# An attention and token/channel mixer on one core: the relative-position bias rectified on one side and read in both directions, rows shifted by the DRAM pitch, and a new order

## The chip, the core and the metric

One core of one Trainium2 chip runs the kernel. The time is the device time of one execution in microseconds; the runs shown are three, and their median is used. A separate execution was profiled.

## The reference, cut to what matters

```python
def _attn_ref(q, k, v, w1, b1, w2):            # (4, 8, 576, 64); hidden 32
    scores = scale * np.matmul(q, k.transpose(0, 1, 3, 2))
    rel = (pos[:, None] - pos[None, :]).astype(np.float32)
    psi_rel = np.log1p(np.abs(rel))
    psi_i = np.log1p(np.maximum(pos[:, None].astype(np.float32), 1.0))
    x = (psi_rel / psi_i)[..., None]
    h = np.maximum(x @ w1 + b1, 0.0)
    bias = h @ w2
    scores = scores + bias.transpose(2, 0, 1)[None, :, :, :]
    scores = scores - np.max(scores, axis=-1, keepdims=True)
    attn = np.exp(scores)
    attn = attn / (np.sum(attn, axis=-1, keepdims=True) + 1e-09)
    return np.matmul(attn, v).astype(np.float32)

def _moe_ref(x, w_tok1, w_tok2, w_ch1, w_ch2): # x: the attention, (4, 576, 512)
    h = np.maximum(x.transpose(0, 2, 1) @ w_tok1, 0.0) @ w_tok2
    u = x + h.transpose(0, 2, 1)
    h2 = np.maximum(u @ w_ch1, 0.0) @ w_ch2
    return (u + h2).astype(np.float32)
```

The bias depends on the row i, on the distance |i - j| and on the head, and on nothing else: for one row it is a function of the distance alone, so the values left of the diagonal are those to the right of it, mirrored.

## The kernel before

**The opening** draws the bias. A table `lw` of log1p(distance), repeated over 128 partitions (4 rows x 32 hidden units), is 1148 columns wide and holds both sides of the diagonal. The 576 x 576 x 8 bias is made in 36 blocks of 16 query rows. For each block four `rectify` steps (L487; L492 on ScalarE, L494 on VectorE) each write 576 columns for four query rows: relu(w1 x log + b1 x psi_i). One of the four goes to ScalarE and three to VectorE. Eight fp32 products of 32 x 288 (L511) apply w2 and put 16 rows x 8 heads on 128 partitions of a PSUM pair; the step `over` (L517) divides by psi_i and copies 576 columns to SBUF, and `put` (L522) sends them to a DRAM tile `bd` (one for each 128 query rows). Beside this, the eight loads of v (L538) and ten products with each (L545) measure v for its scale, the token weights, which come in 64-bit words, are decoded by steps on VectorE (L630, L635, L359), GpSimd (L632, L638) and ScalarE (L634), and k and q are split in a high part (L369, ScalarE) and a rest (`kl`, `ql`, L384, GpSimd).

**Attention** is 16 units (4 pairs of heads, `hp`, by 4 batches) of 5 chunks of query rows. A chunk's scores are products (L783); VectorE adds the bias and takes the row's extreme (L792, the "biased z"); ScalarE takes the exponential (L805); the result is turned by TensorE (L834) with copies of high part and rest (L837, L840), or, for some chunks, split by `rest_hi` (L815, ScalarE) and `rest_lo` (L819 and L384, GpSimd) and turned by a transposing DMA (L823); products with v follow (L861 to L863), then the norm and the token mix, whose stores are L940 (`um`) and L942 (`ul`). The bias of a pair of heads is loaded by `bias_load` (L716 for the four full chunks, L719 twice for the last), once for its four units. The loads of qT, kT (L741) and v (L745) of the next unit are issued by ScalarE's queue, the others by SyncE's.

**The channel part** follows from some 350 us on; the change touches none of its code.

**The order** of all steps is written by a planner, `Plan.order`. It lists for each engine the steps whose inputs are there, takes the engine that could start first, and of the steps that could start within `SLACK` of that the one with the smallest due time (`DUE`); a step in TensorE's present mode gets `STAY` off its due time. `ON` holds costs and preferences for steps that more than one engine can do. The engines then run their instructions in that order, each its own, and wait for one another by semaphores. When TensorE would stand idle in the plan, the planner puts in warming products (L318). DMAs take their semaphores from a ring of eight, so that a DMA is issued only when the one eight before it has landed.

The steps of a block in the opening, as the planner gets them:

```python
rs = [add({"A": 0.68} if g == 3 else {"V": 0.47}, t + DUE["rect"], rectify(hs, g, q0 + 4 * g, 4 * n + g), after=[room], port=True) for g in range(4)]
...
m = add({"T": 1.05}, t + DUE["bmm"], mm, after=rs, take=[ph], free=[hs], mode=3)
...
v_ = add(ON["over"], t + DUE["over"], over, after=[m], take=[eh], free=[ph])
```

## Time and profile before

| | us |
|---|---|
| median of 3 runs | 644.96 |
| lowest, highest | 642.58, 646.78 |
| profiled execution, its own time | 641.31 |
| its span in the profile | 639.4 |
| TensorE busy | 617.8 |
| VectorE busy | 501.8 |
| ScalarE busy | 410.0 |
| GpSimd busy | 266.4 |

The span runs from the first to the last instruction that the profiler shows; 1.9 us of the execution's own time lie around it. An engine's busy time is the union of its instructions, without the issuing of DMAs. A share over the whole span says little here, since the opening, the attention and the channel part have different limits; the stretches have to be read one by one. Rows name the tiles by the program's names; `slots` and `rect` are large tiles that hold many things in turn, so that "rect" in an attention row is a buffer for z. A releaser in brackets is the instruction that ended the idle time before the row.

### The profile page before, as it was taken

The numbers are of one execution on the slowest core, as the hardware profiler recorded it, in microseconds if no ns is written. First come the engines' busy times: TensorE is split into PE (matmuls) and PEld (weight loads), VectorE is DVE, ScalarE is ACT, GpSimd is POOL, SyncE is SP. The second block draws the span as 40 slices with busy tenths as digits, with TensorE's granted clock in tenths as the row PEclk, the third lists the DMA queues.
The fourth block names the chain that finished last, engine by engine and source line by source line (L and its number), as shares of the span: only waits on it lengthen the run. The fifth ranks groups of instructions, "written<-read, shape, count | busy, mean of one in ns | idle before, by whom it ended". The sixth has DMA issues, their size and how long they took to land.

```text
span 639.4 us, 18066 instructions
## 1 busy us (share of the span) xinstructions
PE 617.8 (97%) x7226; PEld 457.3 (72%) x7226; DVE 501.8 (78%) x1242; ACT 410.0 (64%) x751; POOL 266.4 (42%) x299
## 2 busy tenths in 40 slices
PE   9999888998999999999999999999999999999997
PEld 4445777896999998989899874444444468646886
DVE  7998899987899999999999867994775894266222
ACT  7998888876798999989888525542542641244110
POOL 1004777953575888778653700001233422022211
PEclk9999999998999999999999999999999999999999
DMA  8999665798676965466544795664221115400221
GB/s 314 403 365 336 132 143 146 264 332 191 192 160 194 287 125 138 112 144 185 132 95 86 240 290 213 180 176 116 52 64 40 63 34 132 99 1 0 81 86 33
DMA packets 88515, 101.92 MB, mean 159 GB/s; under 512 B 49392, under 2 KB 58864, under 8 KB 88432
## 3 DMA queue, kind: packets, MB, share of 16 engines
q1 hardware_dynamic: 78784, 80.04, 44.6%
q10 hardware_dynamic: 9648, 20.75, 11.1%
q8 instruction: 56, 0.92, 0.6%
q14 instruction: 27, 0.22, 0.1%
HBM read 69.69 MB, written 20.05 MB: 140 GB/s over the span
## 4 chain that ended last, share of the span: by engine, by line
PE 72%; DVE 9%; ACT 7%; DMA 5%; POOL 4%; issue 3%; ACTq 0%; SPq 0%; POOLq 0%; DVEq 0%
PE pair L783 7%; PE bank L834 6%; PE bank L1103 5%; PE bank L1104 5%; PE bank L1102 5%; PE bank L1289 4%; PE bank L1287 4%; PE bank L1288 4%; PE pair L511 4%; DVE z L792 3%; DVE t2a L840 2%; PE pair L1104 2%; PE bank L1195 2%; PE bank L1194 2%; PE pair L1103 2%
## 5 line engine op out<-in xcount | busy, mean ns | idle before, releaser
L805 ACT ACTIVATE z<-z,mx 128x576 f32<-128x576 f32 (+1 forms) x120 | 92.7, 780 | 12.1 <-DVE mx L792 7.6
L792 DVE CUSTOM_DVE_ANT_0 z<-pair,slots 128x576 f32<-128x576 f32 (+1 forms) x120 | 89.3, 756 | 4.2 <-PE pair L783 3.6
L840 DVE SCALAR_TENSOR_TENSOR t2a<-bank,t2a 128x384 f16<-128x384 f32 (+1 forms) x150 | 79.6, 538 | 6.6 <-ACT t2a L837 5.1
L834 PE MATMUL bank<-id,z 128*128 128x128 f32 x469 | 76.0, 283 | 6.2 <-DVE t2a L840 2.7
L837 ACT ACTIVATE t2a<-bank 128x384 f16<-128x384 f32 (+1 forms) x150 | 70.2, 473 | 16.8 <-PE bank L834 11.2
L783 PE MATMUL pair<-kh,qh 64*128 64x288 f32 (+1 forms) x288 | 62.5, 347 | 4.7 <-DVE mx L792 4.0
L834 PEld LDWEIGHTS bank<-id,z 128*128 128x128 f32 x469 | 50.0, 141 | 15.8 <-issue 4.8
L1103 PE MATMUL bank<-slots 128*128 128x512 f16 (+1 forms) x168 | 58.6, 349 | 1.3 <-DMA slots<-wd 1.3
L861 PE MATMUL bank<-vh,t2a 128*128 128x65 f16 x558 | 58.6, 194 | 0.0
L1102 PE MATMUL bank<-slots 128*128 128x512 f16 (+1 forms) x168 | 58.6, 349 | 0.0
L1104 PE MATMUL bank<-slots 128*128 128x512 f16 (+1 forms) x168 | 58.6, 349 | 0.0
L863 PE MATMUL bank<-vh,t2a 128*128 128x65 f16 x558 | 58.2, 192 | 0.1
L862 PE MATMUL bank<-vl,t2a 128*128 128x64 f16 x558 | 58.3, 191 | 0.0
L1298 DVE SCALAR_TENSOR_TENSOR slots<-bank,crow,slots 128x256 f32<-128x256 f32 x42 | 19.6, 481 | 43.2 <-PE bank L1289 34.2
L783 PE MATMUL pair<-kl,qh 64*128 64x288 f32 (+1 forms) x288 | 52.6, 299 | 0.0
L1232 POOL TENSOR_TENSOR me<-me 128x512 f32<-128x512 f16 x12 | 13.6, 1152 | 92.9 <-DVE wd L1078 76.2
L862 PEld LDWEIGHTS <-t2a 128*128 128x128 f16 x558 | 51.2, 98 | 0.6 <-issue 0.2
L861 PEld LDWEIGHTS <-t2a 128*128 128x128 f16 x558 | 51.1, 97 | 0.4 <-issue 0.2
L863 PEld LDWEIGHTS <-t2a 128*128 128x128 f16 x558 | 51.1, 97 | 0.2 <-DVE t2a L840 0.2
L783 PE MATMUL pair<-kh,ql 64*128 64x288 f32 (+1 forms) x288 | 50.9, 292 | 0.0
L783 PEld LDWEIGHTS pair<-kh,qh 64*128 64x128 f32 (+1 forms) x288 | 34.6, 185 | 16.8 <-DVE mx L792 7.6
L1104 PEld LDWEIGHTS <-slots 128*128 128x128 f16 x240 | 23.5, 98 | 24.7 <-issue 1.6
(271 smaller groups left out, 2037.2 us busy)
## 6 DMA issues: line engine op xcount, KB each, us to landing
keep<-wc SPq DMA_DIRECT2D x24, 512.0 KB, 4.2
wd<-wc SPq DMA_DIRECT2D x24, 512.0 KB, 4.7
bd<-slots SPq DMA_DIRECT2D x36, 288.0 KB, 6.4
slots<-bd SPq DMA_DIRECT2D x16, 576.0 KB, 6.9
slots<-v SPq DMA_DIRECT2D x8, 640.0 KB, 8.8
tv<-v ACTq DMA_DIRECT2D x16, 320.0 KB, 3.8
qq<-qT ACTq DMA_DIRECT2D x16, 320.0 KB, 4.2
kk<-kT ACTq DMA_DIRECT2D x16, 320.0 KB, 4.6
```

The source lines that it names most:

```text
L783: PE.matmul(out=pairs[both[h].i][:, 512 - i + n * i:512 + n * i], lhsT=qx[x][w, c * 128:c * 128 + 128], rhs=kx[y][w, k0:k0 + i], start=(j ...
L792: V.tensor_tensor_reduce(out=st["z"][z.i][:, o], in0=pairs[ph.i][:, 512 - i:512 + i], in1=bias_m[hp][:, c, h, :] if c < NCH else bias_l[hp ...
L805: A.activation(out=zz, in_=zz, func=ACTF.Exp, bias=mx_t[z.i][:, h:h + 1], scale=-1.0)
L834: PE.transpose(banks[tb.i][:, n * 128:(n + 1) * 128], st["z"][z.i][:, 384 * i + n * 128:384 * i + (n + 1) * 128], id32)
L837: A.activation(out=block(h.i, 0, m), in_=banks[tb.i][:, 0:128 * m], func=ACTF.Copy, scale=P_SCALE)
L840: V.scalar_tensor_tensor(out=block(h.i, 3, m), in0=banks[tb.i][:, 0:128 * m], scalar=P_SCALE, in1=block(h.i, 0, m), op0=ALU.mult, op1=ALU. ...
L861: PE.matmul(out=o, lhsT=lh, rhs=vh[:, n, 0:D + 1], start=(i == 0), stop=False)
L862: PE.matmul(out=ps[:, h, 0:D], lhsT=lh, rhs=vl[:, n, :], start=False, stop=False)
L863: PE.matmul(out=o, lhsT=ll, rhs=vh[:, n, 0:D + 1], start=False, stop=(i == 4))
L1102: PE.matmul(out=ps, lhsT=w[0][:, c], rhs=uh[:, c], start=(c == 0), stop=False)
L1103: PE.matmul(out=ps, lhsT=w[0][:, c], rhs=ul[:, c], start=False, stop=False)
L1104: PE.matmul(out=ps, lhsT=w[1][:, c], rhs=uh[:, c], start=False, stop=(c == 3))
```

## The change

- `rectify` writes only `far = max(q0 + 16, 576 - q0)` columns, from distance 0 up: the longer of the two sides of the diagonal. The table `lg` is 576 wide and no longer 1148.
- The products read the columns to the right of the diagonal forwards and those to the left of it backwards (step -1), from the same rectified tile. Each row group writes 591 columns (`FOLD`), in which row i of the 16 stands shifted by i columns. A block has cuts at the place where the direction turns and at the border of the PSUM bank: 8 products in 28 blocks, 12 in the other 8.
- `over` copies 591 columns and `put` writes 128 rows of 591 at a pitch of 608 elements. The shift of a row is undone by the load: `bias_rows` reads with a row pitch one element shorter, two pieces of 576 elements for a partition in place of one of 1152.
- v comes a second time, unpadded (`vr`), for its scale: 1152 columns for 1280, nine products for ten.
- The planner counts the ring of eight (`lands`), lets the scores of the first two chunks go ahead of the last product of the bias (`drawn`), and gets new costs, due times, `SLACK` and `STAY`; so the order of all steps is new.

```diff
-TAB = 1148
+FOLD = S + 15
+BP = 608
+BR = NH * BP
-SLACK = 0.099
-STAY = 136.61
+SLACK = 0.095
+STAY = 406.23
...
-       'put': -1632.04,
-       'bl': 332.43,
+       'put': -3146.07,
+       'bl': 136.34,
...
-        wire, port, port_by = 4.0, 0.0, None
+        wire, port, port_by, lands = 4.0, 0.0, None, [0.0] * 4 + [4.0] * 4
...
+                    if s.wire:
+                        t = max(t, lands[0])
...
+                lands = lands[1:] + [s.end]
...
+        def bias_rows(c, i, n, h, m):
+            t = bd[c]
+            return bass.AP(t.tensor, t.offset + 15 + i * (BR - 1) + h * BP, [[BR - 1, n], *([[BP, m]] if m > 1 else []), [1, S]])
...
-        def rectify(h, g, q, k):
+        def rectify(h, g, n, k):
             def do(e):
-                r, win = rect_t[4 * h.i + g], lw[:, 572 - q:572 - q + S]
+                r, win = rect_t[4 * h.i + g][:, 0:n], lw[:, 0:n]
...
-            rs = [add({"A": 0.68} if g == 3 else {"V": 0.47}, t + DUE["rect"], rectify(hs, g, q0 + 4 * g, 4 * n + g), after=[room], port=True) for g in range(4)]
+            far = max(q0 + 16, S - q0)
+            rs = [add({"A": 0.16 + 0.52 * far / S} if g == 3 else {"V": 0.17 + 0.3 * far / S}, t + DUE["rect"], rectify(hs, g, far, 4 * n + g), after=[room], port=True) for g in range(4)]
...
-                for x in range(2):
+                cuts = sorted({0, back_, 512 - w0, FOLD})
+                for a, b in zip(cuts, cuts[1:]):
                     for g in range(4):
-                        PE.matmul(out=pairs[ph.i][NF * g:NF * g + NF, 224 + 288 * x:512 + 288 * x], lhsT=wf.rearrange("p g h -> p (g h)"),
-                                  rhs=rect_t[4 * hs.i + g][:, 288 * x:288 * x + 288], start=True, stop=True)
+                        x = rect_t[4 * hs.i + g]
+                        x = bass.AP(x.tensor, x.offset + abs(a - back_), [x.ap[0], [-1 if a < back_ else 1, b - a]])
+                        PE.matmul(out=pairs[ph.i][NF * g:NF * g + NF, w0 + a:w0 + b], lhsT=wf.rearrange("p g h -> p (g h)"), rhs=x, start=True, stop=True)
...
-                x, y = pairs[ph.i][:, 224:800], eb_t[eh.i]
+                x, y = pairs[ph.i][:, w0:w0 + FOLD], eb_t[eh.i]
...
-                ENG[e].dma_start(out=bd[c][16 * o:16 * o + 16].rearrange("q (h j) -> (q h) j", j=S), in_=eb_t[eh.i])
+                ENG[e].dma_start(out=bass.AP(bd[c].tensor, bd[c].offset + 16 * o * (BR - 1), [[BP, 128], [1, FOLD]]), in_=eb_t[eh.i])
...
-                        for k in range(10):
+                        for k in range(9):
...
-                                      lambda e, c=c: ENG[e].dma_start(out=slots[:, hp % 2, c * PW:(c + 1) * PW], in_=bd[c][:, hp * PW:(hp + 1) * PW]), after=[*bias_s[c], *after])]
+                                      lambda e, c=c: ENG[e].dma_start(out=slots[:, hp % 2, c * PW:(c + 1) * PW].rearrange("p (h j) -> p h j", h=2), in_=bias_rows(c, 0, 128, 2 * hp, 2)), after=[*bias_s[c], *after])]
...
-                lead = chain("scores", add({"T": 0.9 if c < NCH else 0.95}, t + DUE["scores"], scores, after=[*ready, *bias_in[hp, c], drawn],
+                lead = chain("scores", add({"T": 0.9 if c < NCH else 0.95}, t + DUE["scores"], scores, after=[*ready, *bias_in[hp, c], *([drawn] if u or c > 1 else [])],
...
-                    s = add({"A": 0.45}, t + DUE["hi"], rest_hi, after=exps[:1], take=[p2], use=[z])
+                    s = add({"A": 0.45}, t + DUE["hi"], rest_hi, after=[exps[0], drawn], take=[p2], use=[z])
```

In this diff, `back_ = q0 + 15` is the number of columns read backwards, and `w0` the place in the PSUM pair where the 591 columns begin. How the instructions of three places stood and stand follows; the lines of the new file are a few higher (L522 is L535, L716 is L729, L719 is L732, L940 is L953, L632 is L645, L638 is L651, L384 is L389, L819 is L832).

SyncE's queue toward the end of the opening, before: `bd_132` to `bd_136` are the five DRAM tiles of the bias, a row from `slots` is a put (or so many), a row to `slots` a load of the first pair of heads.

```order
L522 DMA bd_133<-slots 128x576 x6
L522 DMA bd_134<-slots 128x576 x4
L716 DMA slots<-bd_132 128x1152
L522 DMA bd_134<-slots 128x576
L716 DMA slots<-bd_133 128x1152
L522 DMA bd_134<-slots 128x576 x3
L522 DMA bd_135<-slots 128x576 x5
L716 DMA slots<-bd_134 128x1152
L522 DMA bd_135<-slots 128x576 x3
L522 DMA bd_136<-slots 128x576 x4
L716 DMA slots<-bd_135 128x1152
```

The same place now:

```order
L535 DMA bd_134<-slots 128x591
L370 DMA keep<-wt 128x1024
L535 DMA bd_135<-slots 128x591 x8
L535 DMA bd_136<-slots 128x591 x2
L729 DMA slots<-bd_132 128x2x576
L535 DMA bd_136<-slots 128x591
L729 DMA slots<-bd_133 128x2x576
L729 DMA slots<-bd_134 128x2x576
L535 DMA bd_136<-slots 128x591
L729 DMA slots<-bd_135 128x2x576
```

The first load of the bias (`bd_132`) stood behind 20 puts, and now stands behind 34 of the 36; the others follow it closely.

GpSimd's queue about the first splits of k and q, before: `keep` is a decode's buffer, `kl_108` and `ql_110` are rests of k and q, `z_118` the first chunk's z.

```order
L611 MEMSET wt2l 128x2x64
L632 TENSOR_SCALAR keep<-keep 128x512
L384 TENSOR_TENSOR kl_108<-kk,kh_107 128x640
L384 TENSOR_TENSOR ql_110<-qq,qh_109 128x640
L819 TENSOR_SCALAR z_118<-z_118 128x384
L384 TENSOR_TENSOR rect<-z_118,rect 128x384
L638 TENSOR_TENSOR slots<-keep 128x512
```

The same place now:

```order
L624 MEMSET wt2l 128x2x64
L651 TENSOR_TENSOR slots<-keep 128x512
L389 TENSOR_TENSOR kl_108<-kk,kh_107 128x640
L645 TENSOR_SCALAR keep<-keep 128x512
L389 TENSOR_TENSOR ql_110<-qq,qh_109 128x640
L737 MEMSET slots 64x64
L738 MEMSET slots 64x64
L651 TENSOR_TENSOR slots<-keep 128x512
L439 MEMSET vh_111 128x10
L440 MEMSET vh_111 64x1
L441 MEMSET vh_111 64x1
L645 TENSOR_SCALAR keep<-keep 128x512
```

The decode step (L632) that stood right ahead of `kl_108` is now L645 and stands eight rows above the piece shown, ahead of the clearing of `vh_113`; two further decodes (L645, L651) stand between the splits and the rows of `z_118`, which come behind seven more rows of clearing (L832, L389).

SyncE's queue at the load of the third pair's bias and the stores of the first token mixes (`um`, `ul`), before:

```order
L823 DMA_TRANSPOSE rect<-rect 128x6x128 x2
L365 DMA keep<-wc 128x1024
L716 DMA slots<-bd_132 128x1152
L716 DMA slots<-bd_133 128x1152
L716 DMA slots<-bd_134 128x1152
L716 DMA slots<-bd_135 128x1152
L719 DMA slots<-bd_136 64x576 x2
L940 DMA um_127<-x_84 128x4x128
L942 DMA ul_130<-x_84 64x128
```

The same place now:

```order
L836 DMA_TRANSPOSE rect<-rect 128x6x128
L729 DMA slots<-bd_132 128x2x576
L729 DMA slots<-bd_133 128x2x576
L953 DMA um_127<-x_84 128x4x128
L955 DMA ul_130<-x_84 64x128
L729 DMA slots<-bd_134 128x2x576
L729 DMA slots<-bd_135 128x2x576
L836 DMA_TRANSPOSE rect<-rect 128x6x128
L370 DMA keep<-wc 128x1024
L732 DMA slots<-bd_136 64x576 x2
L836 DMA_TRANSPOSE rect<-rect 128x6x128
```

The store of `um_127` stood behind all six loads of this bias; now it stands behind two of them, and four come after it.

## Rows read from the trace of the kernel before

**Rows 1.** Page, part 1: busy us (share of the span) xinstructions

```profile
PE 617.8 (97%) x7226; PEld 457.3 (72%) x7226; DVE 501.8 (78%) x1242; ACT 410.0 (64%) x751; POOL 266.4 (42%) x299
```

**Rows 2.** Stretches (start:end, length, then busy PE, PEld, DVE, ACT, POOL, PEclk, DMA, GB/s)

```profile
0.00:57.00 57.00, 53.38 (x692) 26.21 (x692) 50.19 (x120) 52.73 (x80) 2.81 (x18) 1.00 0.97 356
57.00:100.00 43.00, 38.87 (x531) 32.83 (x532) 38.06 (x106) 35.39 (x67) 34.25 (x56) 1.00 0.67 177
100.00:147.00 47.00, 44.16 (x699) 39.68 (x699) 42.98 (x123) 38.32 (x73) 32.60 (x41) 1.00 0.81 256
147.00:157.00 10.00, 6.93 (x68) 5.36 (x68) 6.55 (x17) 6.91 (x13) 3.50 (x4) 0.83 0.95 206
157.00:200.00 43.00, 42.95 (x754) 39.26 (x751) 39.55 (x107) 35.08 (x67) 27.93 (x27) 1.00 0.69 181
...
350.00:635.00 285.00, 283.14 (x1970) 178.33 (x1966) 182.17 (x386) 105.39 (x199) 61.83 (x49) 1.00 0.37 106
```

**Rows 3.** Grouped lines by form, 0 to 60 us: busy us, mean ns

```profile
L517 ACT ACTIVATE slots<-pair,slots 128x576 f32<-128x576 f32 x36 | 26.4, 736 | 0.8 <-PE pair L511 0.2
...
L494 DVE TENSOR_SCALAR rect<-slots 128x576 f32<-128x576 f32 x54 | 24.1, 522 | 0.0
...
L511 PE MATMUL pair<-rect,slots 128*32 128x288 f32 x288 | 21.3, 410 | 1.4 <-ACT slots L517 1.2
...
L492 ACT ACTIVATE rect<-slots 128x576 f32<-128x576 f32 x18 | 13.6, 771 | 0.0
```

**Rows 4.** Timeline of ACT, 0 to 12 us (start us, us, what)

```profile
5.76 1.44 ACT L492 ACTIVATE slots<-slots 128x576 f32<-128x576 f32 x2
```

**Rows 5.** Timeline of PE, 44 to 75 us ([idle before <-releaser])

```profile
57.18 0.39 PE L783 MATMUL pair<-kh,qh 64*128 64x288 f32 x1 [0.39 <-ACT slots L517]
```

**Rows 6.** Timeline of PE, 22 to 32.5 us

```profile
25.57 0.75 PE L545 MATMUL bank<-slots 128*128 128x128 bf16 x10
26.24 2.15 PE L511 MATMUL pair<-rect,slots 128*32 128x288 f32 x32
```

**Rows 7.** DMA, 0 to 57 us (issues: xcount, KB each, median us to landing)

```profile
DMA packets 8937, 20.29 MB, mean 356 GB/s; under 512 B 870, under 2 KB 1126, under 8 KB 8928
...
bd<-slots SPq DMA_DIRECT2D x35, 288.0 KB, 6.4
...
slots<-bd SPq DMA_DIRECT2D x3, 576.0 KB, 6.5
```

**Rows 8.** Grouped lines by form, whole span: exp in two widths

```profile
L805 ACT ACTIVATE z<-z,mx 128x576 f32<-128x576 f32 x106 | 81.4, 774 | 7.6 <-DVE mx L792 7.0 <-DVE sc L596 0.3
...
L805 ACT ACTIVATE z<-z,mx 128x640 f32<-128x640 f32 x14 | 11.6, 826 | 4.5 <-DMA um<-x 3.9 <-DVE mx L792 0.6
```

**Rows 9.** Timeline of DVE, 56 to 61 us

```profile
58.24 0.76 DVE L792 CUSTOM_DVE_ANT_0 z<-pair,slots 128x576 f32<-128x576 f32 x1 [1.11 <-PE pair L783]
```

**Rows 10.** Chain that ended last, 70 to 97 us, its head by line

```profile
by line: POOL ql L384 11.5%; POOL kl L384 11.4%; POOL slots L638 11.0%; POOL vl L384 9.9%; issue 9.7%; PE pair L783 4.3%; DVE keep L630 3.9%; POOL keep L632 3.9%; DVE m L359 3.5%; DVE t2a L840 3.4%; POOL rect L384 3.4%; POOL xl L384 3.2%; P
```

**Rows 11.** Grouped lines by form, 57 to 110 us

```profile
L384 POOL TENSOR_TENSOR kl<-kk,kh 128x640 fp32r<-128x640 f32 x4 | 6.2, 1557 | 1.4 <-ACT rect L837 0.7 <-ACT t2a L837 0.5 <-ACT kh L369 0.2
...
L638 POOL TENSOR_TENSOR slots<-keep 128x512 f32<-128x512 f32 x3 | 3.5, 1162 | 0.0
...
L635 DVE SCALAR_TENSOR_TENSOR keep<-keep 128x512 int32<-128x512 int32 x3 | 2.9, 965 | 0.0
...
L632 POOL TENSOR_SCALAR keep<-keep 128x512 f32<-128x512 f32 x3 | 2.0, 661 | 1.1 <-DVE mxgv L323 1.1
```

**Rows 12.** Timeline of SP, 131 to 150 us

```profile
134.83 1.76 SPq L716 DMA_DIRECT2D slots<-bd  x4
...
138.25 0.48 SPq L940 DMA_DIRECT2D um<-x  x1
```

**Rows 13.** Chain that ended last, 136 to 152 us (start us, us, what)

```profile
138.25 10.53 DMA um<-x
```

**Rows 14.** Timeline of ACT, 146 to 150 us

```profile
149.25 0.83 ACT L805 ACTIVATE z<-z,mx 128x640 f32<-128x640 f32 x1 [3.91 <-DMA um<-x]
```

More of the change, by code (lines that the diff above doesn't have):

```diff
@@ new lines @@
+      'over': {'A': 0.65, 'V': (0.72, 1893.12)},
+      'vh': {'P': (0.7, 1744.94), 'V': (0.4, 999.31), 'A': (0.6, -572.78)},
+      'vl': {'P': (1.36, 1742.79)}}
+DUE = {'tie': 3214.81,
+       'blk': -672.54,
+       'blkn': 50.2,
+       'rect': -472.18,
+       'bmm': -2332.09,
+       'over': -3547.32,
+       'put': -3146.07,
+       'bl': 136.34,
+       'bln': 91.98,
+       'sums': 1443.85,
+       'sumsn': 290.25,
+       'measw': 61.31,
+       'measwn': 81.35,
+       'amax': 622.86,
+       'scales': 365.78,
+       'scalet': -2029.85,
+       'scalec': -785.97,
+       'fill': -1268.45,
+       'fill1': 1424.77,
+       'tok': -986.12,
+       'tokn': 12.44,
+       'dec1': -322.51,
+       'dec2': 676.98,
+       'dec3': 196.27,
+       'dec4': -28.73,
+       'dec5': -1091.05,
+       'load_k': 23.9,
+       'load_q': -1095.84,
+       'split_k': -406.91,
+       'first_k': -128.79,
+       'first_q': -446.99,
+       'split_q': -235.74,
+       'load_v': -1851.82,
+       'prep_v': 3726.37,
+       'prep_vh': -2173.87,
+       'prep_vl': -2860.64,
+       'scores': -148.81,
+       'biased': -160.4,
+       'exp': -560.33,
+       'hi': -929.4,
+       'lo': 287.58,
+       'turn': -239.45,
+       'flip': -605.86,
+       'fliphi': -1578.93,
+       'flip2': -811.41,
+       'fliplo': 61.62,
+       'back': 838.71,
+       'norm': -56.39,
+       'mix0': -1007.88,
+       'mix1': 469.44,
+       'relu': -3392.19,
+       'mix2': -2979.92,
+       'mix2b': -153.48,
+       'store': -1789.73,
+       'w1': 717.8,
+       'w1n': 176.19,
+       'U0': 1280.18,
+       'U0n': -381.53,
+       'U1n': -297.68,
+       'U1': 883.15,
+       'U2': -180.11,
+       'Un': 33.16,
+       'U3': 1371.94,
+       'U4': -465.64,
+       'u1': 1863.2,
+       'u2': -221.98,
+       'u3': -642.62,
+       'u4': -1822.27,
+       'u5': 122.46,
+       'G': 1437.72,
+       'G0': 970.16,
+       'G0n': 43.23,
+       'g1': -1521.12,
+       'g2': 155.66,
+       'ur': 717.4,
+       'H': 2474.54,
+       'e1': 154.26,
+       'e2': -579.53,
+       'e3': -870.28,
+       'e4': 432.52,
+       't2': 1433.37,
+       't3': 155.16,
+       't4': -1001.58,
+       'T1': -1499.32,
+       'Tn': -166.71,
+       'rd': 2012.78,
+       'urs': 350.87,
+       'un': 178.06,
+       'v1': -59.34,
+       'v2': 2407.34,
+       'v3': 41.73,
+       'v4': 1010.47,
+       'v5': -895.21,
+       'v6': -420.54,
+       'v7': -236.11,
+       'v8': -2263.69,
+       'w2m': -62.0,
+       'w2mn': 50.25}
@@ L527, in attention_mixer @@
             overs.append(v_)
-            bias_s.setdefault(c, []).append(add(wire("put", 0.8), t + DUE["put"], put, after=[v_], free=[eh]))
+            bias_s.setdefault(c, []).append(add(wire("put", 0.82), t + DUE["put"], put, after=[v_], free=[eh]))
             bias_all.extend(bias_s[c][-1:])
@@ L537, in load @@
                     def load(e, i=i, h=h):
[L538 removed]
+                        ENG[e].dma_start(out=staging(h.i, 2 * S), in_=vr[i])
                     def sums(e, i=i, h=h):
[L542 to L543 removed]
+                        t = staging(h.i, 2 * S).bitcast(BF16).rearrange("p (n t) -> p n t", t=2)[:, :, 1]
+                        for k in range(9):
                             x = t[:, k * 128:(k + 1) * 128]
[L545 to L547 removed]
+                            PE.matmul(out=banks[vh_.i][:, 0:128], lhsT=x, rhs=x, start=(i == 0 and k == 0), stop=(i == 7 and k == 8))
+                    x = add(wire("sums", 1.51), DUE["sums"] + DUE["sumsn"] * i, load, take=[h])
                     late.append((x, i))
[L549 removed]
+                    last = add({"T": 0.61}, DUE["sums"] + DUE["sumsn"] * i + 6, sums, after=[x, last], take=[vh_] if i == 0 else [], free=[h], use=[vh_])
                     sums_all.append(last)
```

156 lines of the change are left out of this document (26 added, 130 removed).

## The prediction

> **What bounds the kernel now.** I read the busy line of the page first: TensorE is busy 97% of the span, VectorE 78%, ScalarE 64%, GpSimd 42% [rows 1]. So little can be gained by making any other engine cheaper, unless it is the one that TensorE waits for, and the next question is where the missing 3% lie. The table by stretches answers it [rows 2]. From 157 us on TensorE idles 0.05 of 43 us, and 1.9 of the last 285 us; what lies between I take to be of the same kind. The losses are in front: 57.00 - 53.38 = 3.6 us before 57 us, 43.00 - 38.87 = 4.1 to 100 us, 2.8 to 147 us, and 3.1 in the ten microseconds from 147, in which the granted clock is 0.83 besides: a third of that stretch at the lower level (1.2 GHz) costs about 10 x (1 - 0.83) = 1.7 us more. All that a new order can win lies in these four places, some 15 us, since the work behind 157 us is the same and full.
>
> The opening (0 to 57 us) has to be read apart, because TensorE's 53.38 us there are not all work: warming products fill its pauses. In the grouped lines the scaling copy "over" costs ScalarE 736 ns, and it does one rectify of 771 ns in each block; VectorE does three of 522 ns [rows 3] (the row shown is one of two like halves each time: 36 overs, 36 rectifies on ScalarE, 108 on VectorE, 576 matmul records, two to a product). ScalarE starts rectifying at 5.76 us [rows 4] and is busy 52.73 us of the 57 [rows 2]; the first scores wait for its last "over" and start at 57.18 us [rows 5]. VectorE is nearly level (50.19 us busy). TensorE's own share is smaller: two blocks, 32 records, take 2.15 us, so 1.08 a block, and ten products of v for its scale 0.75 including what overlaps, 0.68 from start to start [rows 6]. DMA is at 0.97 in the same stretch, moving 20.29 MB at 356 GB/s [rows 2, 7]. So three resources are within some 10% of each other there, and taking work from one makes the next the bound.
>
> **The change part by part.** All of it is summed against the profiled execution: 641.31 us, of which 639.4 are the span. The median of the runs is 644.96, 3.65 more, and I add that at the end.
>
> *Opening: rectify, copy, products, v unpadded.* A block now rectifies max(q0 + 16, 576 - q0) columns, 440 of 576 in the mean over 36 blocks. ScalarE's slope comes from one line in two widths: 774 ns at 576 columns, 826 at 640 [rows 8], so 52 / 64 = 0.81 ns a column. It saves 136 x 0.81 = 0.110 us x 36 = 4.0; "over" grows by 15 columns, 0.012 x 36 = 0.4; the scaling of the halved table loses 284 columns, 0.2. Together -3.8: the last "over" ends near 53.4 us. VectorE saves in like measure. But the first biased z needs a bias load too. In the old order that load stands behind 20 puts, in the new one behind 34 of 36. Blocks leave ScalarE every (57.2 - 5.8) / 36 = 1.43 us, so the 34th "over" ends near 50.5; put and load take 6.4 to 6.5 us from issue to landing [rows 7], so the load lands near 57.0. On VectorE the first z now also stands behind parts of two decode steps, among them one more operation of 0.965 us and what waits for GpSimd. So z, which began at 58.24 us [rows 9], begins near 57.7: **-0.5**. The floor is -3 (load no longer late, z right behind the products); the ceiling +2 (two decodes of VectorE and GpSimd end first). The bytes say the same: puts grow by 36 x 128 x 15 x 4 = 0.28 MB, v falls by 0.52 and the table by 0.29, so 0.5 MB or 1.5 us at 356 GB/s is all that a DMA-bound opening could give. The 32 products more cost nothing while TensorE's end in the opening (5.8 + 36 x 1.11 + 8 x 0.61 = 50.6 us) is ahead of ScalarE's.
>
> *57 to 100 us: GpSimd's queue.* From 70 to 97 us GpSimd's lines make 54% of the chain [rows 10] (the seven lines of GpSimd that this row names, added). In the old order the splits kl and ql (1.56 us each, ql taken like kl) stand behind a decode step, L632, that VectorE holds until 57 us (the idle time of that line names the releaser, L323 [rows 11]); GpSimd is busy 2.81 us of the first 57 [rows 2]. In the new order what stands ahead of them is released earlier, so they can run inside the opening, and two further decodes (0.661 + 1.162 us each) [rows 11] stand ahead of the first residual of z, which is late anyway. That is 3.1 + 3.6 = 6.7 us less in the chain's stretch at the most; at GpSimd's share 0.54 x 6.7 = **-3.5**. Ends: 0, if the engines beside it (VectorE 38.06 and ScalarE 35.39 of 43 us) become the bound; -6.7, though only 4.1 + 2.8 us of idling can go.
>
> *147 to 157 us: the stall.* SyncE issues four bias loads and two small ones, and the store of the attention's output behind them at 138.25 us [rows 12]; that store lands 10.53 us later [rows 13], and it is what the queue of ScalarE waits for: 3.91 us before it issues the load of qT and goes on with exp [rows 14], because a DMA waits for the one eight before it. In the new order two bias loads stand ahead of that store, and the other two and the small ones behind it and a transpose. With four of six loads gone from in front, the store lands several microseconds earlier, and ScalarE's load has another DMA eight before it. The stall's price is 3.1 idle + 1.7 of clock = 4.8; I take **-4**, ends 0 (another wait of the same ring at the same place) and -4.8.
>
> *What is added.* A bias load is now 128 rows of two pieces of 2304 bytes at a pitch of 2428 and no longer one of 4608; no row shows such a load. From below it costs nothing (the same bytes, hidden behind the full TensorE); from above one stall like the 3.91 us [rows 14]. The same bound holds for the waits on the DMA ring, which the new planner counts but which land elsewhere on the chip than it assumes. I take **+1.0**, nearer to the lower end, since the same bytes are moved and the next set of bias is loaded while TensorE still works on the one before; ends 0 and +4.
>
> No row shows what a start off a boundary costs a transfer. The Trainium skill ("DMA: Bandwidth & Descriptors", section "How a descriptor splits into AXI transactions") speaks against this part: a piece that does not start on a multiple of 256 bytes begins its first transaction at the boundary below, and the bytes before it cost beats too. By it a piece of 72 beats would take about 76, so 5.5% more for 16 loads of 0.59 MB, an estimate of 1.5 us of DMA time spread over the run, most of it hidden; the sum would be +0.5 higher if a third of it showed.
>
> Sum: -0.5 - 3.5 - 4.0 + 1.0 = -7.0, so 634.3 for a profiled execution, and 634.3 + 3.65 = 638.0 against the median. The ends added (-3 - 6.7 - 4.8, and +2 + 4) give 630.5 and 651.
>
> **The rivals.** *A, the gain goes into another wait.* The opening stays bound by DMA (0.97), the moved GpSimd work only delays the first z, and a stall of the same size stands elsewhere on the ring of eight. For it: the DMA share [rows 2] and a load that stands 14 puts later. Against it: the stall was one accident in an otherwise full run. Then 0 to +2 from the opening, -3.5 or 0 behind it, and the stall kept: 641 to 648, in the middle 644.
>
> *B, the order repairs more.* If the opening gives its -3 and the idle time to 147 us falls to a third of its 6.9 us (-4.6), with the stall's -4.8 and nothing added: -12.4, so 632.6.
>
> *C, slower: reading backwards costs TensorE.* In the mean 295 of 591 columns are read with step -1. Nothing in the trace reads with a negative step. Against a price: the products of v read with step 2, at 0.068 us each for 128 columns, 0.53 ns a column [rows 6], where the opening's, at step 1, take 1.08 / 8 / 288 = 0.47; so a step by itself costs next to nothing. If a reversed column costs twice, a block is 1.08 x (591 + 295) / 576 = 1.66 us, 36 of them and 8 x 0.61 us of sums from 5.8 us on end at 70.5 us, 13.3 after the present start of the scores. Then 13.3 - 3.5 - 4 + 1 = +6.8, so 651.8. With a factor f for reversed columns TensorE's end is 50.6 + 19.9 x (f - 1): below f = 1.33 it is hidden behind ScalarE, from f = 1.66 on the kernel is slower than before.
>
> *D, the rectify doesn't shrink with its columns.* Then -3.8 becomes 0 on ScalarE, but the load decided there anyway: 639, inside the forecast's own range.
>
> **How the numbers follow.** A measurement of this kernel tells about 1%, 6.4 us, from no change: faster begins at 638.5. I give the forecast (with D) 0.56, of which 0.36 lies below 638.5 since single terms may well give more or less by 3 us; B 0.10; A 0.22, of which 0.03 is above 651.4; C 0.12, of which 0.09 is. So faster 0.36 + 0.10 = 0.46, slower 0.03 + 0.09 = 0.12, the same 0.42. The range reaches from the lower end of the sum, 630, to just above A, 649; C and the outermost of B are left out.
>
> **What would show it.** Right: ScalarE's rectify at about 0.66 us in the mean and the last "over" near 53.5 us; the first bias load landing at 56 to 58 us and z starting right behind; GpSimd busy some 8 us rather than 2.8 before 57 us, and its share of the chain from 70 to 97 us well below 54%; no idle stretch of TensorE near 150 us and no granted clock under 0.95 there; the same 285 us at the end. Wrong: matmul records of the opening with equal columns but unequal durations (C); a wait of ScalarE or SyncE of over 2 us for a DMA in 60 to 200 us (A); a first z later than 60 us; or a change behind 350 us, which nothing here expects.

## The result, and the profile after

The changed kernel takes 634.53 us (median of 4 runs, 634.4 to 635.4) beside 643.88 (4 runs, 642.58 to 646.78): ratio 0.9852, 95% interval 0.9813 to 0.9890, so 1.5% faster. The forecast was 638.0 with a range of 630 to 649. Its profiled execution took 634.66, its span 632.9.

The busy line of the page answers to [rows 1], the table by stretches, with the same columns, to [rows 2]:

```profile
PE 617.7 (98%) x7302; PEld 456.1 (72%) x7302; DVE 496.3 (78%) x1242; ACT 406.1 (64%) x751; POOL 266.4 (42%) x299
```

```profile
0.00:57.00 57.00, 54.21 (x758) 26.65 (x759) 45.31 (x126) 50.09 (x82) 8.15 (x23) 1.00 0.94 343
57.00:100.00 43.00, 41.15 (x552) 33.95 (x549) 38.59 (x111) 35.66 (x68) 31.56 (x56) 1.00 0.64 195
100.00:147.00 47.00, 45.42 (x763) 41.14 (x762) 42.59 (x117) 39.19 (x74) 31.20 (x39) 1.00 0.95 258
147.00:157.00 10.00, 9.71 (x155) 8.31 (x152) 9.70 (x26) 8.84 (x19) 5.65 (x6) 1.00 0.88 226
157.00:200.00 43.00, 41.20 (x679) 37.16 (x679) 39.56 (x110) 35.96 (x68) 29.07 (x30) 1.00 0.68 176
...
350.00:625.00 275.00, 274.29 (x1838) 170.56 (x1837) 177.18 (x370) 101.99 (x192) 58.05 (x46) 1.00 0.37 106
```

TensorE's idle time (length less busy) is 1.9 us from 57 to 100 us where it was 4.1, 1.6 to 147 us where it was 2.8, and 0.3 in the ten microseconds from 147 where it was 3.1; there the granted clock is 1.00 and no longer 0.83. The first of these falls is no gain by itself: warming products fill 7.28 us of the stretch from 57 to 100 us, and filled 5.14 (the same stretch with the warming line alone, before, then now):

```profile
57.00:100.00 43.00, 5.14 (x41) 3.93 (x41) 1.00 0.67 177
57.00:100.00 43.00, 7.28 (x61) 5.60 (x58) 1.00 0.64 195
```

From 157 to 200 us TensorE idles 1.8 us where it idled 0.05. The last row ends at 625 us, since the span now ends at 632.9; TensorE is as full there as before (273.20 of the same 275 us). GpSimd is busy 8.15 us of the first 57, as forecast. The opening's lines, grouped, answer to [rows 3] (busy us, mean ns; each mean mixes widths now, and the rectify rows are again one half of two):

```profile
L530 ACT ACTIVATE slots<-pair,slots 128x591 f32<-128x591 f32 x36 | 27.2, 757 | 2.8 <-PE pair L525 2.1 <-DVE slots L503 0.2
...
L503 DVE TENSOR_SCALAR rect<-slots 128x544 f32<-128x544 f32 (+17 forms) x54 | 20.5, 442 | 0.4 <-PE pair L525 0.3
...
L501 ACT ACTIVATE rect<-slots 128x544 f32<-128x544 f32 (+17 forms) x18 | 11.7, 662 | 0.0
```

VectorE's rectify fell from 522 to 442 ns, ScalarE's from 771 to 662, and its copy of 591 columns rose from 736 to 757. The copy now also waits 2.1 us in all for the products (0.2 in [rows 3]). Its last one ends 2.4 us earlier, at 54.70 us for 57.13 (ScalarE's timeline, before, then now):

```profile
56.40 0.73 ACT L517 ACTIVATE slots<-pair,slots 128x576 f32<-128x576 f32 x1
53.94 0.76 ACT L530 ACTIVATE slots<-pair,slots 128x591 f32<-128x591 f32 x1 [0.71 <-PE pair L525]
```

Yet the first biased z is not earlier but later. It began at 58.24 us [rows 9]; VectorE's timeline now:

```profile
56.56 0.16 DVE L342 COPY egv<-bank 128x1 f32<-128x1 f32 x1 [1.86 <-PE bank L350]
...
57.44 0.68 DVE L648 SCALAR_TENSOR_TENSOR keep<-keep 128x512 int32<-128x512 int32 x1
59.81 0.43 DVE L643 TENSOR_SCALAR keep<-keep 128x512 int32<-128x512 int32 x1 [1.69 <-POOL slots L651]
...
60.75 0.75 DVE L805 CUSTOM_DVE_ANT_0 z<-pair,slots 128x576 f32<-128x576 f32 x1
```

It stands right behind two operations of a decode (L643, and L364 between the rows shown), and these waited 1.69 us for GpSimd's decode operation (L651). The wait goes further back: L651 needs VectorE's L648, whose input from GpSimd (L645, below) was there at 55.53 us, but which stands in VectorE's order behind the operations on v's scale (L342 and those after it). L342 waited 1.86 us for a small product of TensorE (L350), and ahead of that one stand ScalarE's L349 and 20 warming products (timelines of GpSimd and TensorE):

```profile
54.88 0.65 POOL L645 TENSOR_SCALAR keep<-keep 128x512 f32<-128x512 f32 x1
53.87 2.35 PE L323 MATMUL bank<-ones 128*128 128x256 bf16 x20
```

So the first z begins 6.06 us behind the end of the last `over`, where it was 1.11 us. That distance is the better measure: in the five profiled executions with this opening (this one and, below, E3, E8, its repetition and the control) it is 6.06 us each time, while the last `over` itself ends anywhere from 53.8 to 55.2 us and the first z begins at 59.89 to 61.23. The first bias load was issued at 52.34 us and landed 5.8 us later, at 58.1, so it was no longer what z waited for (SyncE's timeline; the load's own times by its line):

```profile
52.34 0.48 SPq L729 DMA_DIRECT2D slots<-bd  x1
```

```profile
DMA to landing us min/median/max: 5.8/5.8/5.8
```

And the chain from 70 to 97 us, which GpSimd led with 54% [rows 10], is led by VectorE and TensorE:

```profile
by line: DVE z L805 14.7%; PE pair L796 14.4%; issue 12.9%; PE bank L847 6.4%; DVE t2a L853 5.3%; POOL slots L651 5.2%; POOL vl L389 5.0%; DVE rect L805 4.8%; DVE keep L648 4.7%; POOL rect L389 3.4%; DVE m L364 3.0%; POOL tv L764 3.0%; PE b
```

### The profile page after: what moved, and what is told of

Same layout as the page of the kernel before. It is cut to its first block, busy times and chain, and to the rows that moved or that the text cites. A ratio compares the mean times of both kernels' runs of the same rounds, so it can differ in the third digit from the quotient of the medians.

```text
span 632.9 us, 18224 instructions
## 1 busy us (share of the span) xinstructions
PE 617.7 (98%) x7302; PEld 456.1 (72%) x7302; DVE 496.3 (78%) x1242; ACT 406.1 (64%) x751; POOL 266.4 (42%) x299
## 4 chain that ended last, share of the span: by engine, by line
PE 75%; DVE 13%; ACT 3%; DMA 3%; issue 3%; POOL 2%; SPq 0%; DVEq 0%; ACTq 0%; POOLq 0%
PE pair L796 8%; PE bank L847 7%; PE pair L525 4%; PE bank L1116 4%; PE bank L1117 4%; PE bank L1115 4%; PE bank L1300 4%; PE bank L1301 4%; PE bank L1302 4%; DVE z L805 4%; DVE t2a L853 3%; PE pair L1117 2%; PE bank L1206 2%; PE bank L1208 2%; PE pair L1115 2%
```

## The experiments

Each step of the planner's list (2819 in either kernel, of the same kinds) has a number, so an order can be written out and replayed, with its engines, buffers and warming products, in place of the planner's call. That allows one work in the other's order, and single moves. The code and order pieces shown are cuts.

**Work and order, crossed (E1, E2).** The new work in the old order:

```diff
-        for s in plan.order():
+        for i, engine, pad, behind, held in ORDER_OF_BEFORE:
+            s = plan.steps[i]
```

> The new work (one-sided rectify, reversed reading, 591 columns, row shift by pitch, v unpadded) with the steps of the kernel before in the order, on the engines and in the buffers of the kernel before. Theory O (the order made the gain; in the new kernel's trace TensorE's lost time fell at 147 to 157 us and at 57 to 140 us, and rose by 1.5 us before 70 us): the opening of the old order with the new work is shorter by up to 3.8 us on ScalarE, the first biased z starts near 55 us instead of 58.24, and the stall at 147 us stays: 638 to 640 us. Rival W (the work made the gain): about 635. Rival N (misaligned bias loads cost what the opening gives): 641 or more.

Measured: 641.68 (12 runs, 638.99 to 646.12) beside 643.86, ratio 0.9958 (0.9925 to 0.9991). The first z came at 56.39 us, 1.9 earlier than before, and the stall at 147 us was there, longer than before: ScalarE stood 5.1 us before its load of qT, and the granted clock fell twice (timelines of VectorE and ScalarE, table by stretches):

```profile
56.39 0.76 DVE L805 CUSTOM_DVE_ANT_0 z<-pair,slots 128x576 f32<-128x576 f32 x1 [1.15 <-PE pair L796]
```

```profile
149.42 0.36 ACTq L754 DMA_DIRECT2D qq<-qT  x1
149.82 0.83 ACT L818 ACTIVATE z<-z,mx 128x640 f32<-128x640 f32 x1 [5.11 <-DMA um<-x]
```

```profile
100.00:147.00 47.00, 45.48 (x679) 41.11 (x679) 42.32 (x118) 36.94 (x70) 31.77 (x39) 0.93 0.80 243
147.00:157.00 10.00, 5.87 (x49) 4.62 (x46) 5.46 (x16) 6.02 (x12) 2.94 (x4) 0.76 1.16 225
```

The median lies above theory O's range and in rival N's. The four runs with the highest mean granted clock, 0.997, took 638.99 to 640.21, about O's range; the eight others had 0.989 to 0.995.

The old work in the new order, by the same edit to the kernel before:

> The work of the kernel before (two-sided table, 576 columns, one piece of 4608 bytes a partition, v padded) in the order of the new kernel. Theory O: the stall at 147 us is gone, the losses of 70 to 160 us are those of the new kernel, and only the opening is longer, since ScalarE has 3.8 us more to do and the first bias load still stands behind 34 puts: first z at 63 to 64 us, 636 to 638 us in all. Rival W: 641 to 644, as before. If the misaligned loads cost much, this kernel would be faster than the new one, under 634.

Measured: 638.88 (10 runs, 638.31 to 639.86), ratio 0.9922 (0.9897 to 0.9947). The first z came at 65.44 us, 7.2 later than in the old order:

```profile
65.44 0.75 DVE L792 CUSTOM_DVE_ANT_0 z<-pair,slots 128x576 f32<-128x576 f32 x1
```

This is 0.9 us above theory O's range, and far from the 634 that rival N asked for, so N falls. The order is worth 5.0 us on the old work and 641.7 - 634.5 = 7.2 on the new; the work is worth 2.2 in the old order and 4.4 in the new. Theory O holds for the larger share, but the work is no side matter. The order makes the opening 7.2 us longer at the first z and has that back between 132 us and the end of the old order's stall. Where exactly can't be said, since the two orders hand out their z differently: the 37th biased z begins 0.3 us earlier than before (132.38 us, before 132.66), the 46th 3.1 later, the 55th 2.8 earlier. Counted z compare two orders to some 3 us only.

**The stall (E3, E4).** First the new kernel with all six loads ahead of the store again:

```diff
 L729 DMA slots<-bd_133 128x2x576
+L729 DMA slots<-bd_134 128x2x576
+L729 DMA slots<-bd_135 128x2x576
+L732 DMA slots<-bd_136 64x576 x2
 L953 DMA um_127<-x_84 128x4x128
 L955 DMA ul_130<-x_84 64x128
-L729 DMA slots<-bd_134 128x2x576
-L729 DMA slots<-bd_135 128x2x576
...
-L732 DMA slots<-bd_136 64x576 x2
```

> The new kernel with one change of order: the four loads of the third bias set that stood behind the store of um_127 are issued ahead of it, as in the kernel before. Theory S (my prediction's: the store is late because six loads stand ahead of it, and what waits for it stalls): a stall returns, TensorE loses 3 to 5 us between 130 and 155 us, 637 to 640 us. Rival R (the ring of eight: the stall came because ScalarE's load of qT happened to stand eight DMAs behind that store, with exp behind it on ScalarE): ScalarE's loads have other DMAs eight before them here, so no stall, 634 to 635.5.

Measured: 633.46 (6 runs, 632.51 to 634.21). The store lands 9.5 us after its issue, nearly as late as the 10.53 us of [rows 13] and later than the 8.1 us of the new kernel, and TensorE loses nothing by it (the store's line in the new kernel, then here; the stretch):

```profile
DMA to landing us min/median/max: 8.1/8.1/8.1
```

```profile
DMA to landing us min/median/max: 9.5/9.5/9.5
```

```profile
147.00:157.00 10.00, 9.97 (x160) 8.70 (x159) 9.76 (x25) 8.75 (x18) 5.57 (x7) 1.00 0.80 201
```

Theory S falls, and rival R's account holds (the time is even a little under its 634 to 635.5): a late store does no harm while no engine that computes stands eight DMAs behind it; here that place is SyncE's. Then the kernel before, with ScalarE's load of qT moved eight of its steps back and nothing else:

```diff
-L741 DMA qq<-qT 128x640
 L805 ACTIVATE z_118<-z_118,mx_137 128x640
...
 L805 ACTIVATE z_119<-z_119,mx_138 128x576
+L741 DMA qq<-qT 128x640
```

> The kernel before with one change of order: ScalarE issues the load of qT that waited 3.9 us eight steps of ScalarE later, so that exp and copies no longer stand behind it. If that wait was the whole of the stall (rows of 147 to 157 us: 3.1 us of TensorE idle and 1.7 of lower clock), the time falls by 4 to 5 us against the kernel before, to 637 to 639 beside 642 to 644, and the granted clock stays at 1.00 between 147 and 157 us. If the next wait takes its place (um store and turned blocks late as well), it falls by less than 2.

Measured: 638.93 (12 runs, 637.05 to 643.38), ratio 0.9929 (0.9901 to 0.9956), 4.9 us less. The stall is gone; in this execution the clock fell at another place, behind an idle stretch of 1.6 us near 88 us that the kernel before has too, without such a fall:

```profile
57.00:100.00 43.00, 39.29 (x524) 33.52 (x526) 37.33 (x103) 35.03 (x67) 33.81 (x55) 0.96 0.66 177
147.00:157.00 10.00, 9.55 (x123) 8.06 (x121) 9.06 (x25) 8.70 (x17) 4.87 (x5) 1.00 1.10 246
```

So that one wait was worth what the prediction gave it (4.8), and it can be removed by a single move.

**The opening (E5, E6).** Is the later first z on the path? The first z ahead of the decodes:

```diff
+L805 ISA z_118,mx_137<-pair_64,slots 128x576
+L805 ISA z_118,mx_137<-pair_65,slots 128x576
 L648 SCALAR_TENSOR_TENSOR keep<-keep 128x512
 L643 TENSOR_SCALAR keep<-keep 128x512
 L364 TENSOR_REDUCE m_181<-slots 128x1
```

> The new kernel with one change of order: on VectorE the first chunk's two biased z stand ahead of the second and third decode's operations, on ScalarE its exp ahead of the third decode's sign, and the warming products that the planner put ahead of the first two chunks' scores are cut from 17 and 22 to 6 and 4. In the new kernel the first z starts at 60.75 us, right behind a decode operation that waited 1.69 us for GpSimd. Theory D (the decode chain sets the first z, and the delay is on the path): z starts at 58 to 59 us and the run is 1 to 2.5 us shorter, 632 to 633.5 beside 634.5. Rival G (the decodes and splits that then come later on GpSimd take the place, since GpSimd leads the chain behind): z starts earlier, the time stays within 0.7 us of 634.5.

Measured: 635.12 (4 runs, 634.4 to 636.93). z began 4.24 us behind the end of the last `over`, no longer 6.06, so 1.8 us earlier (on the span's time axis 0.6, since the last `over` ended at 55.91 us in this execution). It then waited 1.41 us for a DMA (the first bias load landed at 59.93 us), and the second chunk's z stood behind the decodes instead:

```profile
60.16 0.76 DVE L805 CUSTOM_DVE_ANT_0 z<-pair,slots 128x576 f32<-128x576 f32 x1 [1.41 <-DMA bd<-slots]
```

```profile
57.00:70.00 13.00, 9.65 (x77) 7.02 (x75) 8.13 (x23) 6.38 (x11) 8.14 (x28) 0.94 0.92 319
70.00:100.00 30.00, 28.25 (x391) 23.08 (x389) 28.28 (x82) 26.94 (x53) 23.42 (x27) 0.97 0.52 142
```

With the warming products cut that far the clock fell in this execution, 13 x 0.06 and 30 x 0.03 = 1.7 us, but it is the slowest of the four (636.93): the other three, at mean granted clocks of 0.999 and 1.000, took 634.4 to 635.25. That is rival G's range, no gain. The profile agrees: from the first z to the 17th took 30.5 us, in the new kernel 27.1; of the 3.4 us more 1.7 are clock, and the other 1.7 take back what the first z had won. The decodes are work that has to be done ahead of some chunk, and ahead of the first is no worse. Then the work itself, with one line of it undone:

```diff
-            far = max(q0 + 16, S - q0)
+            far = S
```

> The new kernel, but every rectify writes all 576 columns (the products read the same ones as before); order and bytes are unchanged. The step that exchanged the two works in the new order was worth 638.9 - 634.5 = 4.4 us. Theory A (it is the rectify's columns on ScalarE and VectorE, 4.0 us on ScalarE by my prediction's slope): 638 to 639, first z near 64.5 us. Rival B (it is the 0.8 MB less that v and the table bring through DMA): 634.5 to 635.5.

Measured: 637.79 (4 runs, 637.13 to 638.09), and the first z 4.0 us later:

```profile
64.78 0.75 DVE L805 CUSTOM_DVE_ANT_0 z<-pair,slots 128x576 f32<-128x576 f32 x1
```

Theory A: with 637.8 - 634.5 = 3.3 us the rectify's columns are most of the new work's 4.4, and the delay at the first z is carried on whole (the 45th z is 4.0 later too, 145.49 us for 141.46). What is left, 1.1 us beside E2, is all else that differs, the bytes saved in DMA among it; it was not taken apart.

**GpSimd's queue (E7).** kl and ql behind the first rest of z, and with them the two loads of ScalarE that refill their buffers:

```diff
-L389 TENSOR_TENSOR kl_108<-kk,kh_107 128x640
-L389 TENSOR_TENSOR ql_110<-qq,qh_109 128x640
...
 L389 TENSOR_TENSOR rect<-z_118,rect 128x384
+L389 TENSOR_TENSOR kl_108<-kk,kh_107 128x640
+L389 TENSOR_TENSOR ql_110<-qq,qh_109 128x640
```

> The new kernel with the splits kl and ql of the second unit moved on GpSimd behind the first chunk's rest of z (and the loads of k and q into the freed buffers behind them on ScalarE), so that 3.1 us of GpSimd's work goes from the opening into the stretch in which GpSimd led the chain. My prediction's theory T2 (GpSimd's work in 60 to 100 us costs its share of the chain, 0.54): + 0.54 x 3.1 = 1.7 us, 635.5 to 637. Rival F (the freed GpSimd ends the second decode 3 us earlier, so the first z comes earlier, and that outweighs): 632 to 634. If neither is on the path: 634 to 635.

Measured: 637.13 (6 runs, 636.38 to 639.17). The chain runs through both splits and the decode behind them (start, us, what), TensorE waits 3.1 us for a z (waits: total, times, longest), and the clock falls:

```profile
65.28 1.51 POOL kl L389
66.78 1.49 POOL ql L389
68.27 1.12 POOL slots L651
```

```profile
PE pair L796 <- DVE mx L805: 3.1, 1, 3.1
```

```profile
57.00:100.00 43.00, 38.44 (x476) 31.71 (x473) 34.71 (x98) 33.42 (x63) 33.39 (x55) 0.96 0.57 179
```

The first z stood 6.07 us behind the last `over`, as in the new kernel (6.06), so rival F falls: freeing GpSimd does not bring it forward, since L651 waits for VectorE's L648. (It was 1.0 us earlier only because the last `over` was.) From there to the ninth z took 4.1 us more than in the new kernel, for 3.1 of GpSimd's work, and of that 43 x 0.04 = 1.7 is the clock. That leaves 2.4, a share of 0.77 and not 0.54 in this one case. T2's mechanism holds, and it was sized too small.

**The bias loads (E8).** All pieces on multiples of 256 bytes (BP = 640 for 608; the shift of the rows is left out):

```diff
-            return bass.AP(t.tensor, t.offset + 15 + i * (BR - 1) + h * BP, [[BR - 1, n], ...
+            return bass.AP(t.tensor, t.offset + i * BR + h * BP, [[BR, n], ...
```

> The new kernel with the bias laid at a pitch of 640 elements and its rows not shifted on the way back, so that every piece of 2304 bytes of a put and of a load starts on a multiple of 256 bytes; the same bytes move, at the same places in the order. It leaves out the shift of the rows: the bias that is added is a neighbour's. Theory M (the start off a boundary costs, as the rule in my prediction has it): the bias loads land sooner than the 7.7 us (median of 16) of the new kernel by 5% or more, and the time falls by 0.3 to 1.5 us. Rival H (hidden or free): landings within 5%, 634.2 to 634.8.

Measured: 632.60 (4 runs, 632.27 to 633.0), below both ranges; the 16 loads landed as they did (first the new kernel's, then this one's):

```profile
DMA to landing us min/median/max: 4.3/7.7/12.0
```

```profile
DMA to landing us min/median/max: 4.3/7.8/11.9
```

Time and landings pointed in different directions, so the new kernel went once more beside it, on one chip:

> The new kernel, its steps in the same order, as a control beside the two runs that follow on the same chip. Its four earlier runs gave 634.4 to 635.4, and its profile has a TensorE idle stretch at 183 us (1.5 us lost between 180 and 200 us) that the five other kernels of the new order do not show. If that stretch belongs to the kernel: 634 to 635.5 again. If it was an accident of that execution: 632.5 to 634, and the gain of the kernel with its loads ahead of the store (633.5) is nothing.

> The kernel with aligned bias pieces once more, beside the control on the same chip (it leaves out the shift of the rows, as before). It gave 632.6, 1.9 under the new kernel's earlier runs, but its bias loads landed no sooner (7.8 us against 7.7), and its lead came 0.85 us before the first z and 1.4 at the idle stretch of 183 us. Theory H (alignment free or hidden): within 0.5 us of the control. Theory M (it costs): 1.5 to 2 us under the control.

Measured: control 633.61 (6 runs, 632.53 to 634.94), aligned 632.86 (5 runs, 632.71 to 634.05). What is left is 0.75 us between spreads that overlap, which is neither H's (within 0.5) nor M's (1.5 to 2). The loads landed alike again (the control's, then the aligned kernel's):

```profile
DMA to landing us min/median/max: 4.2/7.9/11.6
```

```profile
DMA to landing us min/median/max: 4.5/7.9/11.9
```

So the cost of the start off a boundary is not settled; it is likely between nothing and some 0.8 us. The control idles only 0.6 us from 157 to 200 us, so 1.2 of the 1.8 us there were an accident of the first profile, and the kernel with its loads ahead of the store (633.46) is as fast as the control.

**A better order (E9, E10).** The opening's last chain shortened on VectorE, with E3's move besides:

```diff
+L648 SCALAR_TENSOR_TENSOR keep<-keep 128x512
 L342 COPY egv<-bank_67 128x1
...
-L648 SCALAR_TENSOR_TENSOR keep<-keep 128x512
```

and on GpSimd the second L651 ahead of ql; warming products 14, 10, 12 for 20, 17, 22. These moves were not tried one by one.

> The new kernel with its opening's last chain shortened and nothing left out: the second decode's VectorE operation stands ahead of the operations on v's scale, its GpSimd operation ahead of the split ql, the warming products ahead of v's scale and of the first two chunks' scores are 14, 10 and 12 for 20, 17 and 22, and the loads of the third bias set stand ahead of the store, as in the run of that name. In the new kernel the first z (60.75 us) waited for that decode, and in the runs with all columns rectified and with the splits moved a delay at the first chunks was carried to the end one for one. Theory E (so is a gain): first z at 58.3 to 59.3 us and 1.5 to 2.5 us under the control. Rival G (GpSimd's queue behind, with ql 1.2 us later, takes it back, as with the decodes behind the first z): within 0.7 us of the control or the loads' run.

Measured: 631.91 (6 runs, 631.44 to 632.46), ratio to the kernel before 0.9826 (0.9801 to 0.9850): the shortest time of all, and 1.7 us under the control on the same chip, as theory E had it; the control's fastest run is slower than the slowest here. First the control's first z, then this kernel's:

```profile
60.11 0.75 DVE L805 CUSTOM_DVE_ANT_0 z<-pair,slots 128x576 f32<-128x576 f32 x1
```

```profile
58.98 0.74 DVE L805 CUSTOM_DVE_ANT_0 z<-pair,slots 128x576 f32<-128x576 f32 x1
```

Of these 1.13 us 0.8 belong to the chain (5.27 us behind the last `over` for 6.06), the rest to an earlier last `over`. L648 came 1.9 us earlier behind it, but VectorE's next decode operation, 0.43 us long in the new kernel, took 1.84 beside GpSimd's ql (56.54 to 58.09 us), here and in the next run:

```profile
56.62 1.84 DVE L643 TENSOR_SCALAR keep<-keep 128x512 int32<-128x512 int32 x1 [0.45 <-POOL slots L651]
```

The lead grew to 1.5 us and fell to 0.5 at 127 us, where ScalarE had a DMA eight places ahead to wait for, this time a bias load:

```profile
125.76 0.34 ACTq L754 DMA_DIRECT2D qq<-qT  x1
...
126.73 0.49 ACT L850 ACTIVATE rect<-bank 128x384 f16<-128x384 f32 x1 [1.96 <-DMA slots<-bd]
```

The profiled executions end 0.9 us apart (631.76, control 632.62), so this lead accounts for a part only of the 1.7 us between the medians.

The last run tried to mend that by moving two loads on ScalarE:

```diff
-L754 DMA qq<-qT 128x640
-L754 DMA kk<-kT 128x640
 L850 ACTIVATE rect<-bank_67 128x384
 L818 ACTIVATE z_120<-z_120,mx_139 128x576
 L850 ACTIVATE t2a_93<-bank_66 128x384
 L374 ACTIVATE vh_111<-tv 128x10x64
+L754 DMA qq<-qT 128x640
+L754 DMA kk<-kT 128x640
```

> The kernel with the shortened opening chain, but with the new kernel's own order of bias loads and store, and with ScalarE's loads of qT and kT near 126 us four steps of ScalarE later. In the kernel with the shortened chain the first z led the control by 1.14 us and the chunks behind it by 1.47, until ScalarE waited 1.96 us at 126 us for a bias load eight DMAs ahead of its load of qT, and the lead fell to 0.5. Theory Q (that wait, with copies queued behind it, took the 1 us): no wait of ScalarE for a DMA over 1 us between 60 and 200 us, the lead stays at 1.4, and the time is 631 to 631.8 beside 631.9. Rival P (TensorE is full from 127 us and the lead is eaten by the next wait anyway): 631.5 to 633, with another idle stretch of about 1 us between 110 and 160 us.

Measured: 637.50 (6 runs, 636.14 to 639.92), 5.6 us more (on another chip; by the ratios to the kernel before, 0.9905 and 0.9826, 5.1), and against both theories. Another load of ScalarE, that of v, now waits for the store of um_127, with a copy queued behind it:

```profile
137.75 0.33 ACTq L758 DMA_DIRECT2D tv<-v  x1
138.19 0.49 ACT L850 ACTIVATE t2a<-bank 128x384 f16<-128x384 f32 x1 [3.85 <-DMA um<-x]
```

```profile
130.00:147.00 17.00, 13.61 (x206) 12.01 (x204) 10.16 (x27) 10.25 (x19) 9.09 (x9) 0.90 1.12 306
```

This is the old stall at a new place: 3.4 us of TensorE idle between 130 and 147 us, and 17 x 0.10 = 1.7 of clock. Two loads moved by four steps brought it back, with the loads and the store in the new kernel's own order: the place on the ring decides.

## Why the prediction was right, and where it was wrong

- *The sum and its reference.* 634.3 was worked out for a profiled execution, and the profiled execution took 634.66. That the two agree so well is in part luck: the errors of the opening and of the stretch behind it roughly cancel, and the control's profiled execution, without the idle stretch at 183 us, took 632.62. What put the forecast 3.5 us above the median is the step "I add that at the end": the 3.65 us by which before's median stood above its profile do not belong to the new kernel. Before's 26 runs beside the first experiments spread from 640.25 to 649.20, at mean granted clocks of 0.986 to 0.996; the new kernel's ten runs lie between 632.5 and 635.4, at 0.998 to 1.000. The old order has long idle stretches, behind which the clock fell in some executions, and the new one has none over 1.1 us; that this is the whole of the spread is argued and not shown.
- *The opening, -0.5.* Measured +2.5 at the first z (+1.7 to +3.0 in the five executions with this opening), one of the prediction's own signs of being wrong ("a first z later than 60 us"). The step that failed is the choice of what is last: I let the bias load decide (57.0, measured 58.1) and put the decode chain at the ceiling of +2; the decode decided, behind v's scale in VectorE's order. Only with the decodes out of the way did a DMA decide (E5). The saving was well sized for the new order, 3.8 on ScalarE against 4.4 us (E2 to the new kernel) and 4.0 at the first z (E6), but the order spends it. In the old order it was 1.9 at the first z (E1), half of it. And `over` now waits 2.1 us for TensorE's products instead of 0.2, which the prediction had put at nothing.
- *57 to 100 us, -3.5.* The mechanism is right (E7), its size is known only roughly: behind its later first z the new kernel is ahead of before by 5.2 us at the 37th z (127.46 us, before 132.66), 3.5 at the 45th (141.46, before 144.94) and 1.9 at the 46th, so it gained 4 to 8 us where 3.5 was put. For the one piece that was moved, the share of the chain was too small (E7). By 147 us -4.0 was forecast, and -2 to -5 came.
- *The stall, -4.* Size right (E4: 4.9; 2.8 of idle and 1.7 of clock in the profiles). Of its two reasons one failed, "the store lands several microseconds earlier": it lands 8.1 us after its issue, 2.4 less than before, but in E3 it takes 9.5 and no one minds. The other, "another DMA eight before it", carries all of it (E3, E10).
- *What is added, +1.0.* Likely between 0 and 0.8 (E8 beside the control). The pitch of the two pieces is 608 elements, so 2432 bytes and not 2428; nothing hangs on it. Of the rule that the Trainium skill gives ("DMA: Bandwidth & Descriptors", section "How a descriptor splits into AXI transactions"), by the prediction's estimate 5.5% more for these loads, the landings show nothing (7.7 us against 7.8 aligned, and 7.9 against 7.9); executions of one order differ by some 4% themselves (7.6 in E3, 7.9 in the control), so the rule is neither shown nor refuted.
- *The rivals.* C is answered by two rows of the new kernel alone, products of 512 columns, forward ones first (the fifth block, at 12 us), then reversed ones (read with step -1, the 33rd block, at 48 us):

```profile
L525 PE MATMUL pair<-slots 128*32 128x512 f32 x8 | 1.2, 601 | 0.0
L525 PE MATMUL pair<-slots 128*32 128x512 f32 x8 | 1.1, 604 | 0.1
```

604 ns against 601: reading backwards has no price here, far from the factor of 1.33 at which the prediction let it show (1.14, had it put in ScalarE's new end, 53.4 us). Its own argument against C was weaker, since it set bf16 products beside fp32 ones. A was wrong here for the time, though SyncE did wait 2.6 and 2.5 us for a DMA between 60 and 200 us, one of the signs named; it came true in E10. B's extra repair did not come at the places named. D fell (rectify 662 ns).

## What to carry to other kernels

An engine that issues DMAs and computes as well is stopped by whichever DMA its next one must follow; look for who stands eight places ahead of each load, not for how early a transfer is issued, and expect that any reordering deals these places anew. A microsecond that work off the critical engine saves can be spent on pulling the next stage's preparation forward: the splits pulled ahead were worth about 3 us here, with the clock's 1.7 (E7), the decodes nothing either way (E5). Take warming products off TensorE's busy time before reading its idle time, and measure a chain from the event that starts it, since the same opening began its first z at 59.9 to 61.2 us. And when runs of a kernel spread above its profile, do not carry the spread over to a kernel without its long idle stretches; here it did not come along.

## What the runs showed that was not expected

The cost of an idle stretch of TensorE was not its length alone. Stretches of 1.6 us (near 88 us, E4), 2.5 (before, 148 us), 3.0 (E10), 3.1 (E7) and 3.7 (E1, 148 us) were followed by time at the lower level: a loss of 1.7 us each time, in E1 of 10 x 0.24 = 2.4 in the row shown and 0.9 more behind it. It did not come every time: the same 1.6 us stretch in the kernel before and one of 1.5 us near 551 us in E2 were followed by none. Nor is it tied to such a stretch: E1 lost another 47 x 0.07 = 3.3 us from 104 us on, where the last stretch of over one microsecond lay at 86 us, and in E5's profile three shorter ones went ahead of it, 0.95, 1.2 and 0.9 us within seven microseconds, where the warming products had been cut. In the new kernel, its control, E3 and E9, where no stretch is longer than 1.1 us, the granted clock stayed at 1.00 in every stretch up to 625 us.
